# Turning attention output by crossbar DMA instead of TensorE in the later units of a fused sparse-attention and gated-FFN kernel

## The chip, the cores and the metric

The kernel runs on one core of one Trainium2 chip. The metric is the device time of one execution in microseconds (us), the median of several. A program on one core has no other core to wait for, so everything that sets the time is in one trace. The trace counts from the first to the last instruction and is about 2 us shorter than the device time: the profiled execution took 268.72 us and its span is 266.7 us.

Names used below: PE is TensorE's matmul side and PEld its weight load, DVE is VectorE, ACT is ScalarE, POOL is GpSimd, SP is SyncE. POOL issues software DMAs (q0), SP issues hardware DMAs (q1), crossbar transposes among them.

## The reference

Two layers, one after the other. The attention has 4 batches, 8 heads, 768 tokens and head size 64. Each query sees its neighbours within 16 positions, and 24 blocks of 32 tokens in a summarised form (keys by maximum, values by mean):

```python
k_sum = k.reshape(B, H, nb, block, D).max(axis=3)       # block = 32, nb = 24
v_sum = v.reshape(B, H, nb, block, D).mean(axis=3)
scores_l = scale * q @ k^T, only where |i - j| < 16
scores_s = scale * q @ k_sum^T + log(block)
a = softmax(concat(scores_l, scores_s));  x = a @ concat(v, v_sum)
```

The output x, as 3072 tokens by 512 features, goes through a gated feed-forward layer with a residual gate:

```python
g = x @ w_gate; val = x @ w_val                          # 512 -> 1536
ffn_out = (gelu(g) * val) @ w_out                        # 1536 -> 512
out = x + sigmoid(x @ w_res) * ffn_out
```

## The kernel before

The work is cut into 8 **units** of 384 tokens (half a batch each, numbered 0 to 7). Heads go in 4 **pairs** of 128 features. In the loop over `u`, the gated layer of unit `u` runs on TensorE with the attention of unit `n = u + 1` woven in, so that TensorE always has matmuls to do. `st` is the state of unit `u`, `nst` that of unit `n`.

Two things have to be turned (transposed) on the way. First, k and q of a batch come in as rows of tokens and are needed with features on the partitions. Second, the normalised attention output `xn` (tokens on partitions) has to become `xT` (features on partitions), since the gated layer contracts over features. TensorE can turn a 128x128 tile into PSUM, from where ACT copies it; SP can issue a crossbar DMA that turns from SBUF to SBUF.

```python
def load_rows(b):                       # rows of k, q (and v) of batch b, cast to bf16, one DMA per head
    for sb, src, name in ((k_sb, k, ..), (q_sb, q, ..), (v_sb, v, ..))[0:2 if b == 1 else 3]:
        ...
        for h in range(H) if b > 1 else (4, 5, 6, 7, 0, 1, 2, 3):
            nc.gpsimd.dma_start(out=sb[b][:, h // 2, :, ...], in_=src[b, h].rearrange("(c p) d -> p c d", c=NC))

def load_batch(b):                      # rows, then the values (vext) in 7 DMAs
    load_rows(b)
    for c in range(NC + 1): load_values(b, c)

def k_step(b, hp, pool, tag):           # turn a pair of k on TensorE: 6 transposes, ACT copy into kW, then
    tp = turn_pair(k_sb[b], hp, pool, tag)
    nc.scalar.copy(kw[:, :, OWN:OWN + QT]..., tp...)
    k_rest(kw)                          # five DVE operations: block maxima and the neighbours' columns
def q_step(...):                        # the same for q: 6 transposes and an ACT copy

def turn_batch(b, p0, p1):              # the same by crossbar DMA: two DMAs for k and one for q of a pair
    for hp in range(p0, p1):
        for e in range(2):
            nc.sync.dma_start_transpose(out=kt[:, :, e, OWN:OWN + QT], in_=k_sb[b][64 * e:64 * e + 64, hp]...)
        nc.sync.dma_start_transpose(out=qT[b % 2][hp]..., in_=q_sb[b][:, hp]...)
def turn_values(b): ...                 # 4 crossbar DMAs, v_sb -> vT, read by block_sums (a DVE reduction, vsT)

def xt_step(u, ko, st, pool, tag, copy):   # a pair of xn: 3 TensorE transposes and an ACT copy
    for sub in range(NSUB):
        nc.tensor.transpose(xp[:, sub * 128:(sub + 1) * 128], st["xn"][:, sub, ko * 128:(ko + 1) * 128], ident[:])
    copy(st["xT"][:, ko, :], xp[:])

def fo_step(st, gvT, fo):               # g and vv: 4 matmuls of 128x384 each (ko 0..3), then gelu (ACT), product (DVE)
def end_step(u, st, sub, c0=0, c1=DM):  # two DVE operations, then the store
    ...
    nc.sync.dma_start(out=out[row:row + 128, c0:c1], in_=o[:, 0:c1 - c0])
```

`ps_mm`, the pool of PSUM banks for g, vv, r and f, has 4 buffers. The loop, with cuts:

```python
for u in range(NU):
    if u == 1: turn_batch(1, 2, NP)                        # k, q of pairs 2 and 3 of batch 1 by crossbar DMA
    for fo in range(FO):                                   # 12 steps
        ... fo_step(st, gvT, fo); values_step(u, fo)       # block_sums, v_spread, vsum_bc at certain steps
        if u == 0 and fo == 4: ...; load_batch(1)
        if u == 2 and fo == 8: gate(gvT[0:1, fo, 0:1]); load_rows(3)     # gate: a POOL copy that waits for gvT
        if half == 0 and 1 < nb < B and fo == 0: vT[nb] = turn_values(nb); turn_batch(nb, 0, NP - 1)
        if half == 1 and 1 < nb < B and fo == 0: turn_batch(nb, NP - 1, NP)
        if half == 1 and 1 < nb < B and 1 < fo < 2 + NP: k_rest(kW[nb % 2][fo - 2])
        if u == 1 and fo == 6: gate(gvT[0:1, fo, 0:1]); load_batch(2)
        if u == 1 and fo in (0, 1, 4, 5): k_step of pairs 0, 1 (fo 0, 1); q_step of pairs 0, 1 (fo 4, 5)
        if u == 1 and fo >= FO - 2: k_rest(kW[1][fo - FO + NP])          # pairs 2, 3
    ...                                                    # u == 0 and u == 7 have their own endings
    s_step(n, 0, nst); s_step(n, 1, nst, ...)              # scores and exp
    res_step(st, 0); ffn_step(st, gvT, 0, 0, FO); res_step(st, 1)
    av_step(n, 0, nst, *AO); av_step(n, 1, nst, *TT)       # weighted values and normalisation: writes xn
    s_step(n, 2, nst); s_step(n, 3, nst, ..., masked=False)
    end_step(u, st, 0); mask_part(3, nst)
    ffn_step(st, gvT, 1, 0, 6);  xt_step(n, 0, ...);  ffn_step(st, gvT, 1, 6, FO);  xt_step(n, 1, ...)
    res_step(st, 2); av_step(n, 2, nst, *AO); av_step(n, 3, nst, *TT); end_step(u, st, 1)
    ffn_step(st, gvT, 2, 0, 7);  xt_step(n, 2, ...);  ffn_step(st, gvT, 2, 7, 10);  xt_step(n, 3, ...)
    ffn_step(st, gvT, 2, 10, FO); end_step(u, st, 2)
```

Of the kernel before, what the change touches and what calls it, by code (L numbers as in the profile page):

```python
# [8 lines left out]
F32 = mybir.dt.float32  # L9
BF16 = mybir.dt.bfloat16  # L10
# [5 lines left out]
def kernel(  # L16
# [86 lines left out]
    with tc.manual_schedule():  # L103
# [61 lines left out]
        def gate(t):  # L165
            nc.gpsimd.tensor_copy(tick[:], t)

        def load_rows(b):
            for sb, src, name in ((k_sb, k, "k_sb"), (q_sb, q, "q_sb"), (v_sb, v, "v_sb"))[0:2 if b == 1 else 3]:
                sb[b] = (qk1 if sb is v_sb else qk).tile([128, NP, NC, 2 * D], BF16, tag=name, name=name)  # L170
                for h in range(H) if b > 1 else (4, 5, 6, 7, 0, 1, 2, 3):
                    nc.gpsimd.dma_start(out=sb[b][:, h // 2, :, h % 2 * D:h % 2 * D + D],  # L172
                                        in_=src[b, h].rearrange("(c p) d -> p c d", c=NC))

# [158 lines left out]
        def av_norm(hp, st):  # L333
            ao = st["ao", hp]
            rz = work.tile([128, NSUB, 2, 1], F32, tag="rz", name="rz")
            nc.vector.reciprocal(rz[:], ao[:, :, :, D:D + 1])  # L336
            xn = st["xn"].rearrange("p s (h d) -> p s h d", d=D)[:, :, 2 * hp:2 * hp + 2, :]
            nc.vector.tensor_mul(xn, ao[:, :, :, 0:D], rz.to_broadcast([128, NSUB, 2, D]))  # L338

        def av_step(u, hp, st, pool=ps_o, tag="ao"):  # L340
# [3 lines left out]
        def xt_step(u, ko, st, pool, tag, copy=nc.vector.tensor_copy):  # L344
            xp = pool.tile([128, TU], BF16, tag=tag, name="xp")
            for sub in range(NSUB):
                nc.tensor.transpose(xp[:, sub * 128:(sub + 1) * 128],  # L347
                                    st["xn"][:, sub, ko * 128:(ko + 1) * 128], ident[:])
            copy(st["xT"][:, ko, :], xp[:])  # L349

        def new_unit():
            return {"xn": upool.tile([128, NSUB, DM], BF16, tag="xn", name="xn"),
                    "xT": upool.tile([128, KO, TU], BF16, tag="xT", name="xT")}

        def half_fo(st, w, fo, lo, hi, acc=None):
# [8 lines left out]
        def fo_end(gvT, fo, g, vv):  # L364
            ge = work.tile([128, TU], F32, tag="ge", name="ge")
            nc.scalar.activation(ge[:], g[:, 0:TU], AF.Gelu)  # L366
            nc.vector.tensor_mul(gvT[:, fo, :], ge[:], vv[:, 0:TU])  # L367
# [29 lines left out]
        def end_step(u, st, sub, c0=0, c1=DM):  # L397
            f, th = st["f", sub], st["th", sub][:, c0:c1]
            nc.vector.scalar_tensor_tensor(th, th, 1.0, f[:, 0:c1 - c0], ALU.add, ALU.mult)  # L399
            o = work.tile([128, DM], F32, tag="o", name="o")  # L400
            nc.vector.scalar_tensor_tensor(o[:, 0:c1 - c0], th, 0.5, st["xn"][:, sub, c0:c1], ALU.mult, ALU.add)  # L401
            row = u * TU + sub * 128
            nc.sync.dma_start(out=out[row:row + 128, c0:c1], in_=o[:, 0:c1 - c0])

        def keep_warm(n, wp=None):
            if wp is None:
# [79 lines left out]
        for u in range(NU):  # L486
            b, half = u // 2, u % 2
            nb = b + 1
            n = u + 1
            if u == 1:  # L490
                turn_batch(1, 2, NP)
            if u == 3:
                for c in range(NC + 1):
                    load_values(3, c)
            gvT = upool.tile([128, FO, TU], BF16, tag="gvT", name="gvT")
            for fo in range(FO):
                if u == 0 and fo < 2:
                    for w, _, acc in firsts[2 * fo:2 * fo + 2]:
                        half_fo(st, w, fo, KO - 1, KO, acc)
                    fo_end(gvT, fo, firsts[2 * fo][2], firsts[2 * fo + 1][2])  # L500
                else:
                    fo_step(st, gvT, fo)
                values_step(u, fo)
                if u == 0 and fo == 4:
                    nc.vector.memset(vsT[:], 0.0)
                    vext_consts(1)
                    kw_consts(1)
                    load_batch(1)
                if u == 2 and fo == 8:
                    gate(gvT[0:1, fo, 0:1])  # L510
                    load_rows(3)
                if half == 0 and 1 < nb < B and fo == 0:
                    vT[nb] = turn_values(nb)
                    turn_batch(nb, 0, NP - 1)
                if half == 1 and 1 < nb < B and fo == 0:
                    turn_batch(nb, NP - 1, NP)
                if half == 1 and 1 < nb < B and 1 < fo < 2 + NP:
                    k_rest(kW[nb % 2][fo - 2])
                if u == 1 and fo == 6:
                    gate(gvT[0:1, fo, 0:1])  # L520
                    load_batch(2)
                if u == 1 and fo in (0, 1, 4, 5):
                    home = TT if fo % 2 else AO
                    if fo < 4:
                        k_step(nb, fo, *home)
                    else:
                        q_step(q_sb[nb], nb, 0, S, fo - 4, *home)
                if u == 1 and fo >= FO - 2:
                    k_rest(kW[1][fo - FO + NP])
                if u == 0 and fo >= FO - 2:  # L530
                    for hp in range(2 * (fo - FO + 2), 2 * (fo - FO + 2) + 2):
                        q_step(qb, 0, TU, S, hp, *(TT if hp % 2 else AO))
            nst = new_unit() if n < NU else None
            if u == 0:
                s_step(n, 0, nst)
                s_step(n, 1, nst, two=(AO, TT))
                r = [res_part(st, sub) for sub in range(NSUB)]
                tanh_part(st, 0, r[0])
                tanh_part(st, 1, r[1])
# [12 lines left out]
                ffn_step(st, gvT, 1, 4, 8)  # L552
                ffn_step(st, gvT, 2, 0, 4)
                xt_step(n, 2, nst, *AO, nc.scalar.copy)
                xt_step(n, 3, nst, *TT, nc.scalar.copy)
                ffn_step(st, gvT, 2, 4, 8)
                for sub in range(NSUB):
                    ffn_step(st, gvT, sub, 8, FO)
                    end_step(u, st, sub)
                st = nst  # L560
                continue
            if nst is None:
                for sub in range(NSUB - 1):
                    res_step(st, sub)
                    ffn_step(st, gvT, sub, 0, FO)
                    end_step(u, st, sub)
                res_step(st, NSUB - 1)
                for c0, c1 in ((0, 256), (256, 384), (384, DM)):
                    ffn_step(st, gvT, NSUB - 1, 0, FO, c0, c1)
                    end_step(u, st, NSUB - 1, c0, c1)  # L570
                continue
            s_step(n, 0, nst)
            s_step(n, 1, nst, two=(AO, TT))
            res_step(st, 0)
            ffn_step(st, gvT, 0, 0, FO)
            res_step(st, 1)
            av_step(n, 0, nst, *AO)
            av_step(n, 1, nst, *TT)
            s_step(n, 2, nst)
            s_step(n, 3, nst, two=(MM, MM), masked=False)  # L580
            end_step(u, st, 0)
            mask_part(3, nst)
            ffn_step(st, gvT, 1, 0, 6)
            xt_step(n, 0, nst, *AO, nc.scalar.copy)
            ffn_step(st, gvT, 1, 6, FO)
            xt_step(n, 1, nst, *TT, nc.scalar.copy)
            res_step(st, 2)
            av_step(n, 2, nst, *AO)
            av_step(n, 3, nst, *TT)
            end_step(u, st, 1)  # L590
            ffn_step(st, gvT, 2, 0, 7)
            xt_step(n, 2, nst, *AO, nc.scalar.copy)
            ffn_step(st, gvT, 2, 7, 10)
            xt_step(n, 3, nst, *TT, nc.scalar.copy)
            ffn_step(st, gvT, 2, 10, FO)
            end_step(u, st, 2)
            st = nst
# [30 lines left out]
```

The softmax here doesn't subtract the row's maximum and nothing guards it: scores larger than these inputs give would overflow.

## Time and profile before

| What | Value |
|---|---|
| time, median of 3 runs (lowest to highest) | 268.97 us (268.72 to 269.71) |
| span of the profiled execution | 266.7 us |
| ACT busy | 136.2 us, 51% |
| POOL busy (mostly issuing DMAs, none after about 133 us) | 93.6 us, 35% |
| DMA queue of POOL (loads, cast to bf16) | 86,032 packets, 16.26 MB |
| DMA queue of SP (crossbar transposes and stores) | 26,464 packets, 11.80 MB |
| TensorE transposes of xn (`xp`, line 347) | 96 |
| crossbar transposes: kW, qT, vT | 20, 10, 8 |

How to read it: matmuls are pipelined, so the duration of one matmul in the profile (326 ns for 128x384) is longer than its share of a dense stream. What a matmul costs in the stream is the distance between starts. An engine that is not the bottleneck may idle for nothing; what counts is a gap on TensorE, and what ended it. The unit of the loop is the natural stage: it begins with the first g product of a unit.

### The profile page before, as it was taken

The page shows a single profiled execution, that of the slowest core. Times are in us where ns is not written, and L with a number is a line of the kernel's source. Part 1 is how long each engine was busy: PE and PEld are TensorE (multiplying, and loading weights), DVE is VectorE, ACT ScalarE, POOL GpSimd, SP SyncE. Part 2 cuts the span into 40 slices and gives each one's busy share as a digit, 9 for nine tenths or more (in the row PEclk, how much of TensorE's full clock was granted, in tenths as well). Part 3 has the DMA queues.
Part 4 walks back from the last instruction along what each step waited for, and adds up shares of the span by engine and source line. Part 5 has one row for each costly group of instructions (what it writes and reads, how often), then busy time and mean ns, then how long its engine had stood idle before and what let it go on. Part 6 is the DMA issues. An engine that isn't in the chain of part 4 may idle for free.

```text
span 266.7 us, 5803 instructions
## 1 busy us (share of the span) xinstructions
PE 253.3 (95%) x2275; PEld 142.9 (54%) x2300; DVE 174.4 (65%) x414; ACT 136.2 (51%) x236; POOL 93.6 (35%) x125
## 2 busy tenths in 40 slices
PE   8799999999999987999799999999999999999995
PEld 2546555566545544556455565556645565556544
DVE  3744853495597858877846789677837863664424
ACT  2756349645365534645265535745365536663310
POOL 7975542990999803999600000000000000000000
PEclk9999999999999999999999999999999999999999
DMA  5999999999999999999990275315001200020012
GB/s 84 170 169 196 197 206 186 136 176 141 165 129 146 177 141 140 129 181 198 155 72 7 106 141 98 68 42 138 0 4 39 81 0 2 0 90 32 0 42 79
DMA packets 112523, 28.43 MB, mean 107 GB/s; under 512 B 98672, under 2 KB 109552, under 8 KB 112496
## 3 DMA queue, kind: packets, MB, share of 16 engines
q0 software_dynamic: 86032, 16.26, 81.5%
q1 hardware_dynamic: 26464, 11.80, 21.4%
q8 instruction: 18, 0.29, 0.5%
q14 instruction: 9, 0.07, 0.1%
HBM read 32.51 MB, written 6.29 MB: 145 GB/s over the span
## 4 chain that ended last, share of the span: by engine, by line
PE 79%; DMA 9%; DVE 7%; issue 3%; ACT 1%; POOL 1%; DVEq 0%; POOLq 0%
PE f L394 22%; PE vv L360 19%; PE g L360 18%; PE r L378 7%; PE ao L328 3%; DMA vT<-v_sb 3%; DMA qa<-in_q_dram 3%; DMA kW<-k_sb 3%; PE s L296 3%; DVE gvT L367 2%; PE xp L347 2%; PE vs L254 1%; PE wp L409 1%; DVE vext L274 1%; DVE vsT L239 1%
## 5 line engine op out<-in xcount | busy, mean ns | idle before, releaser
L366 ACT ACTIVATE ge<-g 128x384 f32<-128x384 f32 x95 | 46.7, 491 | 66.4 <-PE g L360 37.1
L360 PE MATMUL vv<-xT,w_val 128*128 128x384 bf16 x380 | 77.8, 326 | 2.6 <-DVE gvT L367 2.6
L360 PE MATMUL g<-xT,w_gate 128*128 128x384 bf16 x380 | 77.8, 326 | 1.5 <-DVE gvT L367 1.5
L367 DVE TENSOR_TENSOR gvT<-ge,vv 128x384 bf16<-128x384 f32 x95 | 51.8, 550 | 31.7 <-PE vv L360 28.3
L394 PE MATMUL f<-w_out,gvT 128*128 128x512 bf16 (+2 forms) x298 | 68.6, 362 | 0.7
L360 PEld LDWEIGHTS <-w_val 128*128 128x128 bf16 x384 | 37.5, 98 | 28.7 <-issue 4.2
L360 PEld LDWEIGHTS <-w_gate 128*128 128x128 bf16 x384 | 37.0, 98 | 26.7 <-issue 2.2
L394 PEld LDWEIGHTS <-gvT 128*128 128x128 bf16 x312 | 27.6, 98 | 25.6
L349 ACT COPY xT<-xp 128x384 bf16<-128x384 bf16 x32 | 15.1, 481 | 22.6 <-PE xp L347 22.6
L378 PE MATMUL r<-w_res,xT 128*128 128x512 bf16 x88 | 23.6, 380 | 0.6 <-issue 0.3
L399 DVE SCALAR_TENSOR_TENSOR th<-th,f 128x512 f32<-128x512 f32 (+2 forms) x26 | 16.7, 641 | 11.4 <-PE f L394 8.5
L99 POOL DMA_DIRECT2D vext<-in_v_dram x28 | 23.3, 870 | 2.1 <-PE g L360 1.7
L172 POOL DMA_DIRECT2D k_sb<-in_k_dram x24 | 20.0, 850 | 10.2 <-DMA w_out<-in_moe_w_out_dram 5.2
L384 ACT ACTIVATE th<-r 128x512 f32<-128x512 f32 x24 | 14.2, 602 | 17.9 <-PE r L378 17.9
L313 DVE TENSOR_TENSOR P<-P,maskt 128x768 bf16<-128x768 bf16 x28 | 15.4, 555 | 10.0 <-ACT P L305 7.7
L172 POOL DMA_DIRECT2D q_sb<-in_q_dram x24 | 20.0, 856 | 0.4 <-DMA k_sb<-in_k_dram 0.2
L338 DVE TENSOR_TENSOR xn<-ao,rz 128x384 bf16<-128x384 f32 x32 | 17.8, 557 | 1.1
L305 ACT ACTIVATE P<-s,bias_t 128x768 bf16<-128x768 f32 x18 | 16.2, 903 | 3.8 <-PE s L296 3.7
L401 DVE SCALAR_TENSOR_TENSOR o<-th,xn 128x512 f32<-128x512 f32 (+2 forms) x26 | 16.9, 650 | 0.9
L336 DVE RECIPROCAL rz<-ao 128x6 f32<-128x6 f32 x32 | 6.1, 190 | 15.7 <-PE ao L328 15.7
L302 ACT ACTIVATE P<-s,bias_t 128x384 bf16<-128x384 f32 x28 | 14.6, 578 | 0.0
L172 POOL DMA_DIRECT2D v_sb<-in_v_dram x16 | 13.2, 869 | 0.2 <-issue 0.2
(82 smaller groups left out, 212.5 us busy)
## 6 DMA issues: line engine op xcount, KB each, us to landing
out_dram<-o SPq DMA_DIRECT2D x23, 256.0 KB, 2.1
vext<-in_v_dram POOLq DMA_DIRECT2D x20, 128.0 KB, 7.8
k_sb<-in_k_dram POOLq DMA_DIRECT2D x24, 96.0 KB, 6.1
q_sb<-in_q_dram POOLq DMA_DIRECT2D x24, 96.0 KB, 4.3
w_gate<-in_moe_w_gate_dram POOLq DMA_DIRECT2D x6, 256.0 KB, 8.9
w_val<-in_moe_w_val_dram POOLq DMA_DIRECT2D x6, 256.0 KB, 9.1
w_out<-in_moe_w_out_dram POOLq DMA_DIRECT2D x3, 512.0 KB, 14.1
v_sb<-in_v_dram POOLq DMA_DIRECT2D x16, 96.0 KB, 6.3
```

The lines of the kernel that those rows point to most:

```text
L99: nc.gpsimd.dma_start(out=dst, in_=v[b, :, lo:hi, :].rearrange("h p d -> p h d"))
L172: nc.gpsimd.dma_start(out=sb[b][:, h // 2, :, h % 2 * D:h % 2 * D + D], in_=src[b, h].rearrange("(c p) d -> p c d", c=NC))
L305: nc.scalar.activation(P.rearrange("p a t q -> p a (t q)"), s[:, :, 0:TU], AF.Exp, scale=scale, bias=bias_t[:])
L313: nc.vector.tensor_mul(Pf, Pf, maskt.unsqueeze(1).to_broadcast([128, 2 * HT, QT]))
L338: nc.vector.tensor_mul(xn, ao[:, :, :, 0:D], rz.to_broadcast([128, NSUB, 2, D]))
L360: nc.tensor.matmul(acc[:, 0:TU], w[:, ko, fs], st["xT"][:, ko, :], start=(ko == 0), stop=(ko == KO - 1))
L366: nc.scalar.activation(ge[:], g[:, 0:TU], AF.Gelu)
L367: nc.vector.tensor_mul(gvT[:, fo, :], ge[:], vv[:, 0:TU])
L378: nc.tensor.matmul(r[:], st["xT"][:, ko, ss], w_res[:, ko, :], start=(ko == 0), stop=(ko == KO - 1))
L394: nc.tensor.matmul(st["f", sub][:, 0:c1 - c0], gvT[:, fo, ss], w_out[:, fo, c0:c1], start=(fo == 0), stop=(fo == FO - 1))
L399: nc.vector.scalar_tensor_tensor(th, th, 1.0, f[:, 0:c1 - c0], ALU.add, ALU.mult)
L401: nc.vector.scalar_tensor_tensor(o[:, 0:c1 - c0], th, 0.5, st["xn"][:, sub, c0:c1], ALU.mult, ALU.add)
```

## The change

For units 4 to 7 the first three pairs of the attention output are turned by crossbar DMA instead of TensorE and ACT. That DMA takes time to land, so the first three products of these units contract pairs 0, 1 and 3 first and pair 2 last; pair 3 stays on TensorE. `xn` is laid out by pairs so that the source of a transpose is contiguous. So that SP's in-order queue doesn't hold the transposes behind stores, the stores of units 3 to 6 go by POOL's software queue. In return the crossbar no longer turns k and q of pairs 2 and 3 of batch 1: TensorE turns all four pairs of them in unit 1, the heads are loaded in plain order, and the load of batch 2 is issued at the start of unit 1 with no gate.

```diff
-                for h in range(H) if b > 1 else (4, 5, 6, 7, 0, 1, 2, 3):
+                for h in range(H):
...
+        def xt_dma(ko, st):
+            nc.sync.dma_start_transpose(out=st["xT"][:, ko, :].rearrange("d (s m) -> d s m", s=NSUB),
+                                        in_=st["xn"][:, ko].rearrange("p s d -> p (s d)"))
...
-            return {"xn": upool.tile([128, NSUB, DM], BF16, tag="xn", name="xn"),
+            return {"xn": upool.tile([128, KO, NSUB, 128], BF16, tag="xn", name="xn"),
...
-            nc.sync.dma_start(out=out[row:row + 128, c0:c1], in_=o[:, 0:c1 - c0])
+            (nc.gpsimd if 2 < u < NU - 1 else nc.sync).dma_start(out=out[row:row + 128, c0:c1], in_=o[:, 0:c1 - c0])
...
             if u == 1:
-                turn_batch(1, 2, NP)
+                load_batch(2)
...
+            if u > 3:
+                firsts = [(w, fo, ps_mm.tile([128, 512], F32, tag="mm", name="gv"))
+                          for w, fo in ((w_gate, 0), (w_val, 0), (w_gate, 1))]
+                for kos in ((0, 1, 3), (2,)):
+                    for w, fo, acc in firsts:
+                        for ko in kos:
+                            nc.tensor.matmul(acc[:, 0:TU], w[:, ko, ...], st["xT"][:, ko, :],
+                                             start=(ko == 0), stop=(ko == 2), skip_group_check=True)
...
-                if u == 1 and fo == 6:
-                    gate(gvT[0:1, fo, 0:1])
-                    load_batch(2)
-                if u == 1 and fo in (0, 1, 4, 5):
+                if u == 1 and fo < 8:
                     home = TT if fo % 2 else AO
-                    (k_step of pairs 0, 1 at fo 0, 1; q_step of pairs 0, 1 at fo 4, 5)
-                if u == 1 and fo >= FO - 2:
-                    k_rest(kW[1][fo - FO + NP])
+                    (k_step of pairs 0 to 3 at fo 0 to 3; q_step of pairs 0 to 3 at fo 4 to 7)
...
+            if u < 3:  (the ending as before)
+            else:
+                xt_dma(0, nst)
+                xt_dma(1, nst)
+                mask_part(3, nst)
+                end_step(u, st, 0)
+                ffn_step(st, gvT, 1, 0, FO)
+                av_step(n, 2, nst, *AO)
+                xt_dma(2, nst)
+                av_step(n, 3, nst, *TT)
+                res_step(st, 2)
+                end_step(u, st, 1)
+                ffn_step(st, gvT, 2, 0, 10)
             xt_step(n, 3, nst, *TT, nc.scalar.copy)
             ffn_step(st, gvT, 2, 10, FO)
             end_step(u, st, 2)
```

The lines in brackets stand for code that is cut.

More of the change, by code (lines that the diff above doesn't have):

```diff
@@ L336, in av_norm @@
             nc.vector.reciprocal(rz[:], ao[:, :, :, D:D + 1])
-            xn = st["xn"].rearrange("p s (h d) -> p s h d", d=D)[:, :, 2 * hp:2 * hp + 2, :]
+            xn = st["xn"][:, hp].rearrange("p s (h d) -> p s h d", d=D)
             nc.vector.tensor_mul(xn, ao[:, :, :, 0:D], rz.to_broadcast([128, NSUB, 2, D]))
@@ L347, in xt_step @@
                 nc.tensor.transpose(xp[:, sub * 128:(sub + 1) * 128],
-                                    st["xn"][:, sub, ko * 128:(ko + 1) * 128], ident[:])
+                                    st["xn"][:, ko, sub, :], ident[:])
             copy(st["xT"][:, ko, :], xp[:])
+        def xt_dma(ko, st):
+            nc.sync.dma_start_transpose(out=st["xT"][:, ko, :].rearrange("d (s m) -> d s m", s=NSUB),
+                                        in_=st["xn"][:, ko].rearrange("p s d -> p (s d)"))
         def new_unit():
-            return {"xn": upool.tile([128, NSUB, DM], BF16, tag="xn", name="xn"),
+            return {"xn": upool.tile([128, KO, NSUB, 128], BF16, tag="xn", name="xn"),
                     "xT": upool.tile([128, KO, TU], BF16, tag="xT", name="xT")}
@@ L400, in end_step @@
             o = work.tile([128, DM], F32, tag="o", name="o")
-            nc.vector.scalar_tensor_tensor(o[:, 0:c1 - c0], th, 0.5, st["xn"][:, sub, c0:c1], ALU.mult, ALU.add)
+            nc.vector.scalar_tensor_tensor(o[:, 0:c1 - c0].rearrange("p (k d) -> p k d", d=128),
+                                           th.rearrange("p (k d) -> p k d", d=128), 0.5,
+                                           st["xn"][:, c0 // 128:c1 // 128, sub, :], ALU.mult, ALU.add)
             row = u * TU + sub * 128
-            nc.sync.dma_start(out=out[row:row + 128, c0:c1], in_=o[:, 0:c1 - c0])
+            (nc.gpsimd if 2 < u < NU - 1 else nc.sync).dma_start(out=out[row:row + 128, c0:c1], in_=o[:, 0:c1 - c0])
         def keep_warm(n, wp=None):
@@ L495 @@
             gvT = upool.tile([128, FO, TU], BF16, tag="gvT", name="gvT")
+            if u > 3:
[4 more added lines that the diff above has]
+                        for ko in kos:
+                            nc.tensor.matmul(acc[:, 0:TU], w[:, ko, fo * 128:(fo + 1) * 128], st["xT"][:, ko, :],
+                                             start=(ko == 0), stop=(ko == 2), skip_group_check=True)
             for fo in range(FO):
@@ L500 @@
                     fo_end(gvT, fo, firsts[2 * fo][2], firsts[2 * fo + 1][2])
+                elif u > 3 and fo == 0:
+                    fo_end(gvT, fo, firsts[0][2], firsts[1][2])
+                elif u > 3 and fo == 1:
+                    fo_end(gvT, fo, firsts[2][2], half_fo(st, w_val, fo, 0, KO))
                 else:
@@ L518 @@
                     k_rest(kW[nb % 2][fo - 2])
-                if u == 1 and fo == 6:
-                    gate(gvT[0:1, fo, 0:1])
-                    load_batch(2)
-                if u == 1 and fo in (0, 1, 4, 5):
+                if u == 1 and fo < 8:
                     home = TT if fo % 2 else AO
-                    if fo < 4:
-                        k_step(nb, fo, *home)
-                    else:
-                        q_step(q_sb[nb], nb, 0, S, fo - 4, *home)
-                if u == 1 and fo >= FO - 2:
-                    k_rest(kW[1][fo - FO + NP])
+                    hp, kq = fo % NP, fo // NP
+                    if kq:
+                        q_step(q_sb[nb], nb, 0, S, hp, *home)
+                    else:
+                        k_step(nb, hp, *home)
                 if u == 0 and fo >= FO - 2:
@@ L580 @@
             s_step(n, 3, nst, two=(MM, MM), masked=False)
[L581 to L593, printed above, removed]
+            if u < 3:
+                end_step(u, st, 0)
+                mask_part(3, nst)
+                ffn_step(st, gvT, 1, 0, 6)
+                xt_step(n, 0, nst, *AO, nc.scalar.copy)
+                ffn_step(st, gvT, 1, 6, FO)
+                xt_step(n, 1, nst, *TT, nc.scalar.copy)
+                res_step(st, 2)
+                av_step(n, 2, nst, *AO)
+                av_step(n, 3, nst, *TT)
+                end_step(u, st, 1)
+                ffn_step(st, gvT, 2, 0, 7)
+                xt_step(n, 2, nst, *AO, nc.scalar.copy)
+                ffn_step(st, gvT, 2, 7, 10)
+            else:
+                xt_dma(0, nst)
+                xt_dma(1, nst)
+                mask_part(3, nst)
+                end_step(u, st, 0)
+                ffn_step(st, gvT, 1, 0, FO)
+                av_step(n, 2, nst, *AO)
+                xt_dma(2, nst)
+                av_step(n, 3, nst, *TT)
+                res_step(st, 2)
+                end_step(u, st, 1)
+                ffn_step(st, gvT, 2, 0, 10)
             xt_step(n, 3, nst, *TT, nc.scalar.copy)
```

## The prediction

> **What bounds the kernel now.** I read first the busy shares and the chain of the page, to find the engine that sets the end:
>
> ```profile
> PE 253.3 (95%) x2275; PEld 142.9 (54%) x2300; DVE 174.4 (65%) x414; ACT 136.2 (51%) x236; POOL 93.6 (35%) x125
> ...
> PE 79%; DMA 9%; DVE 7%; issue 3%; ACT 1%; POOL 1%; DVEq 0%; POOLq 0%
> ```
>
> TensorE is busy 95% of the span and 79% of the chain. So there are two ways to gain: fewer instructions on TensorE, or shorter gaps on it, which are 266.7 - 253.3 = 13.4 us in all. The view by windows, cut at the first g product of each unit, shows where the gaps lie (columns: window, its length, busy time of PE, PEld, DVE, ACT, POOL with their counts, then clock, DMA share, GB/s):
>
> ```profile
> 54.80:87.34 32.54, 32.05 (x281) 18.25 (x283) 24.58 (x58) 17.49 (x31) 25.92 (x33) 1.00 1.92 152
> 87.34:119.62 32.28, 29.54 (x255) 16.36 (x257) 25.03 (x46) 16.24 (x29) 19.87 (x25) 1.00 1.81 153
> 119.62:150.24 30.62, 28.92 (x250) 16.23 (x252) 20.42 (x50) 15.64 (x28) 10.80 (x14) 1.00 1.38 105
> 150.24:179.50 29.26, 29.00 (x254) 16.39 (x256) 23.74 (x46) 16.19 (x29) 0.00 (x0) 1.00 0.46 96
> 179.50:208.41 28.91, 28.75 (x250) 16.25 (x252) 19.78 (x50) 15.68 (x28) 0.00 (x0) 1.00 0.16 42
> 208.41:237.28 28.87, 28.71 (x250) 16.25 (x252) 17.89 (x36) 15.64 (x28) 0.00 (x0) 1.00 0.07 28
> ```
>
> These are units 1 to 6. Units 5 and 6 are dense: 0.16 us of gap each. Unit 2 has 32.28 - 29.54 = 2.74 us of gap and unit 3 has 1.70 us. Unit 1 is long because it has more matmuls, and has 0.49 us of gap. Then I asked DVE's waits what made the gaps:
>
> ```profile
> DVE vsT L239 <- DMA vT<-v_sb: 3.4, 2, 2.2
> DVE km L206 <- DMA kW<-k_sb: 1.2, 1, 1.2
> ```
>
> In unit 2, DVE waits for the crossbar transpose of v before the block sums. The products gvT stand behind these in DVE's queue, and TensorE waits for their PSUM banks. In unit 3 the same comes of the last pair of k. In both cases the transposes were slow because POOL's loads were in flight. The first vT, issued at 89.6 us, landed after 8.5 us; in unit 4, with no loads, the same transposes landed in 2.8 us.
>
> **What the Trainium skill says.** "VectorE: DVE Perf Modes", section "The three transpose paths", gives 390 ns for a 128x128 transpose on TensorE and 1309 ns on the crossbar. Here a lone TensorE transpose shows 219 ns, and three of them between matmuls cost 0.17 us, that is 57 ns each in the stream. For the crossbar this trace shows 1.2 us of issue and 2.8 us to landing for six tiles at once. "DMA: Bandwidth & Descriptors", section "Issuing engines are not separate DMA queues", says DMAs of all issuers run on the same 16 engines and interleave; the 8.5 us against 2.8 us agrees. "SBUF — State Buffer", section "Who interferes with whom", says a DVE copy in a two-port mode and GpSimd block each other. The same column copy (L210) took 0.48 us while POOL was issuing at 58.57 us, and 0.20 us at 60.47 us after POOL had stopped. That agrees, though it is no proof of the cause.
>
> **Part 1: k and q of pairs 2 and 3 on TensorE, unit 1.** Four more turns of 6 transposes are 24 x 57 ns = **+1.37 us** on TensorE. ACT gets four more copies of 0.80 us; with one gelu of 0.49 us a step that is 1.3 us, under the 1.64 us that TensorE then needs for a step (8 x 163 ns + 6 x 57 ns). DVE is nearer the limit. Its five operations for a pair of k now come in four consecutive steps, and this is how the first two went:
>
> ```profile
> 57.25 0.55 DVE L367 TENSOR_TENSOR gvT<-ge,vv 128x384 bf16<-128x384 f32 x1
> 57.72 0.35 DVE L206 TENSOR_TENSOR km<-kW 128x384 bf16<-128x384 bf16 x1
> 58.10 0.55 DVE L208 TENSOR_REDUCE ks<-km 128x24 bf16<-128x384 bf16 x1
> 58.57 0.48 DVE L210 COPY kW<-kW 128x176 bf16<-128x176 bf16 x1
> 58.69 0.41 DVE L211 COPY kW<-kW 128x176 bf16<-128x176 bf16 x1
> 59.02 0.21 DVE L212 COPY kW<-ks 128x288 bf16<-128x288 bf16 x1
> 59.16 0.54 DVE L367 TENSOR_TENSOR gvT<-ge,vv 128x384 bf16<-128x384 f32 x1
> ```
>
> From one gvT to the next is 1.91 us, so DVE loses 0.27 us a step, 1.1 us over four. The four PSUM banks let vv of step fo + 2 run once gvT of step fo is done. By these starts vv of step 4 begins at about 62.0 us and needs gvT 2 at 61.5; vv of step 6 begins at 65.3 us and needs gvT 4 at 65.3. So TensorE is touched only at the end: +0.3 us. The two pairs' operations that stood at steps 10 and 11 are gone from there, which may give back up to 0.3 us (one wait of TensorE for a masked P, 0.2 us). Unit 1: **+1.4 us**.
>
> **Part 2: the earlier load of batch 2.** Before, POOL idled from 59.56 us (end of the values of batch 1) to the gate at 66.12 us. Without the gate the 31 loads start 6.6 us earlier, and issue back to back at 0.83 us each, if their completions allow it. Before, the last values were issued at 90.8 to 92.3 us, across the start of vT's transposes. In the changed kernel they go out by about 85.7 us. Unit 2 starts at about 88.8 us, and the transposes of v come 2.2 us later, behind the last store. They then find few loads in flight and should land in 3 to 5 us, before the block sums of step 5 at about 98 us. The gap of unit 2 should shrink to what unit 4, the same code with no loads, shows: 0.26 us. **-2.5 us** in the gap; with fewer slowed DVE copies I take -2.6 us.
>
> **Part 3: unit 3.** The load of batch 3 is gated on step 8 of unit 2 in both kernels. It takes some 28 us of issue, and the last pair of k is turned 2 us into unit 3, some 20 us after the gate: still among the loads. I keep 1.4 of the 1.7 us gap: **-0.3 us**.
>
> **Part 4: xT by crossbar, endings of units 3 to 6.** Each loses 9 transposes: 9 x 57 ns = 0.51 us, four times: **-2.05 us**. The question is whether pair 2 lands in time. In the ending of unit 5, moved to the new order, TensorE does 12 f matmuls from 201.08 us (216 ns each), then the values of pair 2 by 203.95. DVE does the mask of pair 3 (to 203.4), the two operations of the end (0.69 us each, to 204.8), the reciprocal and xn, done by 205.6. Six tiles land in 2.8 us; three tiles, an estimate from that, in about 2.5: 208.2 us. The new first products start at 207.8 us; 9 matmuls x 163 ns later, at 209.26, pair 2 is needed. Slack is 1 us. Pair 3 is tighter: its ACT copy ends about 208.05 us and its first matmul is due at 208.13. I add +0.3 us over all four units for these. Stores by POOL (0.33 us of issue on SP before, 2.0 us to landing) may overlap the transpose; they are 256 KB in 2 KB rows, so I expect tenths of a microsecond, inside the slack.
>
> **The sum:** +1.4 - 2.6 - 0.3 - 2.05 + 0.3 = -3.25 us, so 268.97 - 3.25 = **265.7 us**, 1.2% faster.
>
> **Rivals.**
> First, **the earlier load only moves the queue**. The page shows DMA engines at 9 tenths through units 0 to 2. If they are truly full, loads land no earlier, vT waits as before, and part 2 gives nothing: about 268.3 us. For it: the digit. Against it: POOL issued loads from 66 us on with no wait, and q's landed in 3.3 to 3.9 us there, so the engines kept up; and six crossbar transposes leave unit 1.
> Second, **pair 2 lands late**. If a transpose beside a store takes 5 us, TensorE waits some 1.5 us in each of four units: +6 us, 271.7 us. For it: loads stretched transposes to 7 and 8 us. Against it: those were long trains of packets under 512 bytes, and one store is 2 us of large ones.
> Third, **DVE becomes the bound of unit 1**. If POOL's issuing slows each pair's operations to 2.4 us a step, DVE loses 3 us over four steps and TensorE waits some 2 us: 267.5 us.
> Fourth, **unit 3's gap vanishes too**, if loads of batch 3 get ahead: 264.3 us.
>
> **Range and chances.** The savings on TensorE (2.05 us) and the cost (1.37 us) are counted instructions and nearly sure; unit 2's gap is the largest uncertain term (0 to -2.7 us), then lateness of pair 2 (0 to +6, most likely under 0.5), unit 1 (0 to +2) and unit 3 (0 to -1.7). Together 263.7 to 268.3 us, 8 times in 10. Over 2% faster means under 263.6 us: all terms good at once. Over 2% slower, over 274.3 us, would need the second rival at its worst.
>
> **What would show it.** Right: unit 1 some 33.9 us long; unit 2 about 29.6 us with DVE no longer waiting for vT; units 5 and 6 about 28.4 us, with no wait of TensorE for xT at the first products; unit 3 still waiting for kW. Wrong: a wait "gv from DMA xT" in units 4 to 7; gvT late in steps 3 to 6 of unit 1; vT still landing in over 6 us in unit 2; or unit 4 slowed, where SP issues 13 other transposes.

## The result, and the profile after

The changed kernel takes 264.75 us (264.24 to 265.45) against 269.33 us for the kernel before, timed beside it. The ratio is 0.9834, 95% interval 0.9802 to 0.9866: 1.7% faster. The span went from 266.7 to 262.5 us.

The busy shares and the chain of waits of the changed kernel, from its page:

```profile
PE 251.4 (96%) x2263; PEld 142.0 (54%) x2288; DVE 174.8 (67%) x414; ACT 133.2 (51%) x228; POOL 100.1 (38%) x136
...
PE 86%; DMA 6%; POOL 3%; issue 1%; DVE 1%; ACT 1%; POOLq 0%; DVEq 0%
```

TensorE is busy 1.9 us less, and its share of the chain rose from 79 to 86%, DVE's fell from 7 to 1%. So 4.2 - 1.9 = 2.3 us, more than half of what the span gained, are waits that went. TensorE's waits for the product gvT, behind which a PSUM bank comes free, fell from 4.1 to 1.2 us (two lines of before, one of after; us in total, times, longest):

```profile
PE vv L360 <- DVE gvT L367: 2.6, 4, 1.1
PE g L360 <- DVE gvT L367: 1.5, 1, 1.5
PE g L364 <- DVE gvT L371: 1.2, 1, 1.2
```

The windows, cut at the first product of units 1 to 6 (window, its length, busy time of PE, PEld, DVE, ACT, POOL, then clock, DMA share, GB/s), say where:

```profile
54.82:88.10 33.28, 33.12 (x305) 19.50 (x307) 25.25 (x58) 20.30 (x35) 30.15 (x37) 1.00 1.83 142
88.10:117.40 29.30, 29.04 (x254) 16.39 (x256) 24.92 (x46) 16.25 (x29) 15.76 (x20) 1.00 1.61 154
117.40:147.12 29.72, 28.37 (x242) 15.75 (x244) 20.18 (x50) 14.31 (x25) 10.88 (x15) 1.00 1.77 112
147.12:175.91 28.79, 28.53 (x245) 15.88 (x247) 23.75 (x46) 14.79 (x26) 1.63 (x4) 1.00 0.61 107
175.91:204.30 28.39, 28.23 (x242) 15.76 (x244) 19.74 (x50) 14.22 (x25) 1.65 (x4) 1.00 0.21 54
204.30:232.70 28.40, 28.24 (x242) 15.74 (x244) 17.91 (x36) 14.19 (x25) 1.62 (x4) 1.00 0.12 39
```

| Unit | before, us | after, us | difference | predicted |
|---|---|---|---|---|
| 1 | 32.54 | 33.28 | +0.74 | +1.4 |
| 2 | 32.28 | 29.30 | -2.98 | -2.6 |
| 3 | 30.62 | 29.72 | -0.90 | -0.3 (gap) - 0.51 (transposes) |
| 4 | 29.26 | 28.79 | -0.47 | -0.51 |
| 5 | 28.91 | 28.39 | -0.52 | -0.51 |
| 6 | 28.87 | 28.40 | -0.47 | -0.51 |

What stands before unit 1 is the same (54.80 and 54.82 us). The last unit is 0.38 us longer, all of it after TensorE's last matmul; more on that below. The sum is -4.2 us, the difference of the spans.

In the view of DVE's waits, the line of `vsT` that waited for vT is gone. The one of `km` stays:

```profile
DVE km L206 <- DMA kW<-k_sb: 1.1, 1, 1.1
```

### The profile page after: what moved, and what is told of

It is laid out like the page before. It is cut to its first block, busy times and chain, and to the rows that moved or that the text cites. A ratio compares the mean times of both kernels' runs of the same rounds, so it can differ in the third digit from the quotient of the medians.

```text
span 262.5 us, 5776 instructions
## 1 busy us (share of the span) xinstructions
PE 251.4 (96%) x2263; PEld 142.0 (54%) x2288; DVE 174.8 (67%) x414; ACT 133.2 (51%) x228; POOL 100.1 (38%) x136
## 4 chain that ended last, share of the span: by engine, by line
PE 86%; DMA 6%; POOL 3%; issue 1%; DVE 1%; ACT 1%; POOLq 0%; DVEq 0%
PE f L398 23%; PE vv L364 21%; PE g L364 20%; PE r L382 8%; PE ao L328 4%; PE gv L508 3%; DMA vext<-in_v_dram 3%; DMA kW<-k_sb 3%; PE s L296 2%; POOL vext L99 2%; PE xp L347 1%; PE tp L185 1%; PE vs L254 1%; PE gv L364 1%; POOL k L90 1%
## 5 line engine op out<-in xcount | busy, mean ns | idle before, releaser
L364 PE MATMUL vv<-xT,w_val 128*128 128x384 bf16 x364 | 74.5, 326 | 0.0
L370 ACT ACTIVATE ge<-g 128x384 f32<-128x384 f32 x87 | 42.8, 492 | 59.5 <-PE g L364 33.9
L364 PE MATMUL g<-xT,w_gate 128*128 128x384 bf16 x348 | 71.3, 326 | 1.2 <-DVE gvT L371 1.2
L371 DVE TENSOR_TENSOR gvT<-ge,vv 128x384 bf16<-128x384 f32 x91 | 49.6, 551 | 27.9 <-PE vv L364 26.3
L398 PE MATMUL f<-w_out,gvT 128*128 128x512 bf16 (+2 forms) x298 | 66.6, 362 | 0.7
L364 PEld LDWEIGHTS <-w_val 128*128 128x128 bf16 x368 | 36.0, 98 | 24.5 <-issue 0.9
L364 PEld LDWEIGHTS <-w_gate 128*128 128x128 bf16 x352 | 33.8, 98 | 23.3 <-issue 1.8
L409 POOL DMA_DIRECT2D out_dram<-o x12 | 6.6, 546 | 98.8 <-DVE rz L336 83.9
L398 PEld LDWEIGHTS <-gvT 128*128 128x128 bf16 x312 | 28.3, 98 | 28.2
L349 ACT COPY xT<-xp 128x384 bf16<-128x384 bf16 x20 | 9.3, 482 | 17.5 <-PE xp L347 17.5
```

The costliest lines, as they stand in the source:

```text
L364: nc.tensor.matmul(acc[:, 0:TU], w[:, ko, fs], st["xT"][:, ko, :], start=(ko == 0), stop=(ko == KO - 1))
L398: nc.tensor.matmul(st["f", sub][:, 0:c1 - c0], gvT[:, fo, ss], w_out[:, fo, c0:c1], start=(fo == 0), stop=(fo == FO - 1))
```

## The experiments

Lengths of units are compared where the clock of the window is 1.00. In some profiles TensorE ran at a lower clock for a few microseconds, in the first 20 us or after a gap; the last section says what the traces show of this.

### Was it the earlier load of batch 2? The gate put back

```diff
-            if u == 1:
-                load_batch(2)
...
+                if u == 1 and fo == 6:
+                    gate(gvT[0:1, fo, 0:1])
+                    load_batch(2)
```

> The changed kernel with the load of batch 2 put back behind its gate at step 6 of unit 1; everything else stays. Theory A (the load that starts 7 us earlier closed the gap of unit 2): the transposes of v meet the loads again and land in 6 to 9 us, unit 2 grows from 29.3 to about 31.8 us, the time from 264.8 to about 267.3 us. Rival B (the six crossbar transposes that left unit 1 freed the DMA engines, and the gate did not matter): unit 2 stays under 30 us and the time at about 265 us.

Measured: 268.63 us, 0.9971 of the kernel before (0.9947 to 0.9995). Its second unit, in the view by windows, and DVE's wait:

```profile
89.18:121.53 32.35, 29.54 (x254) 16.37 (x256) 25.52 (x46) 16.21 (x29) 20.28 (x26) 1.00 1.74 155
```

```profile
DVE vsT L239 <- DMA vT<-v_sb: 2.9, 1, 2.9
```

The gap is back (2.81 us), and so is the wait for vT, whose transposes landed after 5.8 to 9.3 us instead of 2.8 to 5.0. The unit is as long as before the change, although the six crossbar transposes of unit 1 were gone here. Rival B falls: without the earlier load the gap stays. The time is 1.3 us above theory A's number. This profile is 1.1 us longer before unit 1, at a lower clock, but the 14 runs at a clock of 0.999 or more have a median of 268.4 us too, so the clock does not explain it; what does stays open.

### Is the earlier load enough? It alone, on the kernel before

```diff
             if u == 1:
                 turn_batch(1, 2, NP)
+                load_batch(2)
...
-                if u == 1 and fo == 6:
-                    gate(gvT[0:1, fo, 0:1])
-                    load_batch(2)
```

> The kernel before with one edit: the load of batch 2 at the start of unit 1, ungated; k and q of pairs 2 and 3 stay on the crossbar and xT stays on TensorE. Theory A (the earlier load closes the gap of unit 2): unit 2 falls from 32.3 to about 29.7 us, unit 1 stays at 32.3 to 32.8 us, time about 266.5 us. Rival B (fewer crossbar transposes in unit 1 did it): unit 2 stays at about 32 us and the time near 269 us; the crossbar transposes of unit 1 might also land too late for the scores, which would lengthen unit 1.

> The kernel before with the early ungated load of batch 2 alone, once more, since the clock of TensorE was lowered to 0.95 in units 2 and 3 of its first profile. If the six crossbar transposes of unit 1 slow the loads enough that these end 4 us into unit 2 (as in the first profile), the gap of unit 2 is again 2 to 3 us and the time 268 to 269 us. If the loads end by the start of unit 2, the gap is under 0.6 us and the time about 266.5 us.

Measured: 267.73 us, ratio 0.9947 (0.9926 to 0.9969), and the second time 267.55 us, 0.9941 (0.9916 to 0.9965). In the first profile the values went out only at 91.24 us, 4.1 us into unit 2; DVE waited 3.7 us for vT, and TensorE 2.56 us for gvT, after which its clock was lower for some 4 us. Where the load came out so late, it gained nothing. The second profile has the full clock; its unit 2 and the wait:

```profile
87.18:117.76 30.58, 29.67 (x258) 16.36 (x256) 24.56 (x46) 16.23 (x29) 18.06 (x24) 1.00 1.66 154
```

```profile
DVE vsT L239 <- DMA vT<-v_sb: 1.7, 1, 1.7
```

There the load alone shortens unit 2 by 1.7 us of the 3.0. Neither number of the second expectation is right: the gap is 0.91 us, between the under 0.6 and the 2 to 3 that it named. The medians put the gain in time at 1.3 and 1.5 us (269.0 and 269.09 us for the kernel before). POOL's timeline shows why. In the profile of the changed kernel its values go out like this (start, length, engine, line, count):

```profile
68.73 6.58 POOL L172 DMA_DIRECT2D q_sb<-in_q_dram  x8
75.22 6.86 POOL L172 DMA_DIRECT2D v_sb<-in_v_dram  x8
82.02 5.79 POOL L99 DMA_DIRECT2D vext<-in_v_dram  x7
```

With the early load but the crossbar transposes of k and q still in unit 1 (second profile), q's loads wait for older loads to complete, and the last values go out later:

```profile
75.22 0.82 POOL L172 DMA_DIRECT2D q_sb<-in_q_dram  x1 [0.62 <-DMA k_sb<-in_k_dram]
76.24 1.64 POOL L172 DMA_DIRECT2D q_sb<-in_q_dram  x2 [0.20 <-issue]
77.86 3.31 POOL L172 DMA_DIRECT2D v_sb<-in_v_dram  x4
81.40 3.28 POOL L172 DMA_DIRECT2D v_sb<-in_v_dram  x4 [0.23 <-DMA q_sb<-in_q_dram]
84.65 5.77 POOL L99 DMA_DIRECT2D vext<-in_v_dram  x7
```

There they are out at 90.42 us, here at 87.81. The bracket on a line names what POOL waited for.

### Both at once: k and q of pairs 2 and 3 back on the crossbar

```diff
             if u == 1:
+                turn_batch(1, 2, NP)
                 load_batch(2)
...
-                if u == 1 and fo < 8:
+                if u == 1 and fo in (0, 1, 4, 5):
...
+                if u == 1 and fo >= FO - 2:
+                    k_rest(kW[1][fo - FO + NP])
```

> The changed kernel with k and q of pairs 2 and 3 of batch 1 back on the crossbar (heads 4 to 7 loaded first, block maxima at steps 10 and 11), the early ungated load kept. If the two parts are independent: unit 1 falls from 33.3 to about 32.4 us and unit 2 stays at 29.3, time about 264.0 us, a version faster than both. Rival (the crossbar transposes of unit 1 and the early load share the DMA engines and hinder each other): unit 2's gap comes back in part or the scores of unit 2 wait at the end of unit 1, time 265 to 266.5 us.

Measured: 266.85 us, ratio 0.9883 (0.981 to 0.9956). Unit 1 falls to 32.55 us, 0.73 less than in the changed kernel, as expected. But unit 2 is 29.84 us with a gap of 0.55, DVE waits 1.0 us for vT, and unit 3 is 30.26 us with DVE waiting 2.0 us for kW. What unit 1 gives, units 2 and 3 take back: 0.54 + 0.54 us. Unit 1 also starts 1.3 us later in this profile, at a lower clock before it. That is not why the median is 2.1 us over the changed kernel's: the two runs with the clock at 0.999 are the longest of the four (267.14 and 268.25 us), and with four runs this stays open. The parts are not independent, and this version isn't shown to be better.

Six profiles stand in one order, by how long after the start of unit 2 POOL was done with issuing the values:

| Kernel | values issued by, against the start of unit 2 | length of unit 2, us |
|---|---|---|
| before | 92.26 - 87.34 = +4.9 us | 32.28 |
| gate put back | 94.01 - 89.18 = +4.8 us | 32.35 |
| earlier load alone, first profile | 91.24 - 87.10 = +4.1 us | 33.71, about 1.7 of it matmuls at half speed after the gap |
| earlier load alone, second profile | 90.42 - 87.18 = +3.2 us | 30.58 |
| k and q back on the crossbar | 90.82 - 88.64 = +2.2 us | 29.84 |
| changed | 87.81 - 88.10 = -0.3 us | 29.30 |

The transposes of v, issued some 2.2 us into the unit, come late as far as the loads of the values overlap them. The three profiles with the earlier load and the crossbar transposes run the same program up to there, save for the layout of xn, so their spread is one of executions: the removed gate takes 0.8 to 2.7 us off that overlap. With the six crossbar transposes out of unit 1 besides, the spread is gone: in the seven other profiles that have both edits and the same ending of unit 2, the values are out 0.4 to 1.6 us before unit 2 and it takes 29.29 to 29.30 us. Against the second profile of the load alone, the loads end 2.6 us earlier in the changed kernel, and the unit starts 0.9 us later, most of it TensorE's added work. That added work is what pays for the rest of the gain.

### xT on TensorE again

```diff
-            if u < 3:
+            if u < NU:
                 end_step(u, st, 0)
```

with the plain order of the first products and all stores on SP.

> The changed kernel with x of all pairs turned on TensorE again in the endings of units 3 to 6, the plain order of the first products, and all stores on SP; the early load and TensorE's k and q of unit 1 stay. Theory C (the gain of these units is the 9 transposes of 57 ns that TensorE no longer does): units 3 to 6 longer by 0.5 us each, time about 266.8 us. Rival D (something else helped there, as the ACT copies that went or the stores that moved): the units change by clearly less or more than 0.5 us each. If the last unit, 29.80 us long in the changed kernel against 29.42 before, goes back to 29.4, the POOL stores made its tail longer.

Measured: 266.26 us, ratio 0.9858 (0.9779 to 0.9937). Units 4 to 6 of this kernel:

```profile
147.13:176.43 29.30, 29.04 (x255) 16.38 (x256) 23.76 (x46) 16.24 (x29) 0.00 (x0) 1.00 0.48 96
176.43:205.30 28.87, 28.71 (x251) 16.25 (x253) 19.79 (x50) 15.65 (x28) 0.00 (x0) 1.00 0.16 42
205.30:234.17 28.87, 28.71 (x251) 16.25 (x253) 17.90 (x36) 15.64 (x28) 0.00 (x0) 1.00 0.08 28
```

They are 0.51, 0.48 and 0.47 us longer than in the changed kernel, which is 9 transposes of 57 ns. TensorE's busy time differs by as much (0.51, 0.48, 0.47 us) and its gaps by nothing, so the ACT copies and the stores, which this run undoes as well, have no part in it. In unit 3 the difference is 0.25 us, because the gap there differs too; that is one reason why the time is under the 266.8 us expected. Theory C holds for units 4 to 6. The last unit is 29.83 us with all stores on SP, so POOL's stores are not what makes its tail longer. Over all profiles the last unit takes 29.35 to 29.83 us, and no run separated a cause.

### The stores back on SP

```diff
-            (nc.gpsimd if 2 < u < NU - 1 else nc.sync).dma_start(out=out[...], in_=o[...])
+            nc.sync.dma_start(out=out[...], in_=o[...])
```

> The changed kernel with the stores of units 3 to 6 back on SP's queue; the transposes of xn stay there too. The change moved the stores so that SP, which issues in order, would not hold a transpose behind a store. Theory E (the order in the program already keeps the transposes ahead: the first store is ready about 0.8 us before xn of pair 2, and a store takes 0.33 us of SP): no wait appears, units 3 to 6 stay within 0.1 us, time within 0.5 us of the changed kernel. Rival F (the stores hold the transposes): a wait of TensorE for xT of pair 2 at the first products of units 4 to 7, 0.5 to 1.5 us each, time up to 4 us more.

Measured: 264.02 us, ratio 0.983 (0.9794 to 0.9866), the same as the changed kernel's. SP's timeline at the end of unit 5 shows the order that the program gives:

```profile
200.73 0.33 SPq L409 DMA_DIRECT2D out_dram<-o  x1
201.43 1.18 SPq L352 DMA_TRANSPOSE xT<-xn  x1
```

The first store is issued 0.7 us before the third transpose, which waits for xn, not for the store. Units 4 and 5 are 28.79 and 28.37 us. Unit 6 is 28.53, 0.13 more than in the changed kernel: the first matmul of pair 2 starts 0.2 us after its turn there. With the stores on POOL the same unit varies from 28.40 to 28.82 us, so this is no cost of SP. Moving the stores to POOL brought nothing.

### The plain order of the first products

The edit takes out the block `if u > 3: firsts = ...` and its two branches at steps 0 and 1.

> The changed kernel with the plain order of the first products (pairs 0, 1, 2, 3, one product after the other) in units 4 to 7. In the trace of the changed kernel the last of the three transposes of a unit is issued 2.4 us before its first product and lands 2.3 us after issue when no store is in flight, up to 4.1 us beside one. Theory G (the reordering is needed): TensorE waits 0.3 to 1.5 us for xT of pair 2 at the first g of units 4 to 7, time 1 to 4 us more. Rival H (it lands in time anyway): units within 0.1 us of the changed kernel.

Measured: 266.30 us, ratio 0.9906 (0.9876 to 0.9935). TensorE's timeline at the start of unit 6:

```profile
204.88 0.49 PE L364 MATMUL g<-xT,w_gate 128*128 128x384 bf16 x2
206.56 0.48 PE L364 MATMUL g<-xT,w_gate 128*128 128x384 bf16 x2 [1.20 <-DMA xT<-xn]
```

After pairs 0 and 1 it waits 1.20 us for pair 2. In unit 4 it waits 0.35 us, in units 5 and 7 not at all. Both theories were too simple: the order is needed in some units. The third transpose was issued at 202.5 us and took 4.1 us to land. In the changed kernel it took 3.9 us at this place (issued at 201.9 us), and by the starts in the windows above pair 2 was due there 9 x 163 ns after 204.3 us, at 205.8. The reordering is worth just what that landing needs.

### The same for unit 3, among loads

```diff
-            if u < 3:
+            if u < 2:
...
-            if u > 3:
+            if u > 2:
```

> The changed kernel with xT of pairs 0 to 2 by crossbar one unit more, for unit 3 as well (the ending of unit 2), where the loads of batch 3 are in flight. If loads stretch these transposes as they stretched those of k and v (7 to 9 us to landing instead of 2.4), TensorE waits 2 to 5 us at the first products of unit 3 and the time is 266.5 to 269.5 us: then the change stops at unit 4 because of the loads. If the transposes land in under 4 us in spite of the loads, the time falls by another 0.5 us to about 264.2 us.

Measured: 267.47 us, ratio 0.9934 (0.9912 to 0.9957). The three transposes landed after 6.5 to 7.7 us, and TensorE's waits show

```profile
PE gv L508 <- DMA xT<-xn: 3.5, 2, 2.3
```

both at the start of unit 3. Unit 2 is 0.44 us shorter (28.86), unit 3 is 34.02 us, part of that at a lower clock after these gaps. This is the prediction's second rival one unit earlier, with loads in the place of the store: beside loads the crossbar is late, which is a reason for the change to stop at unit 4.

### The last pair of batch 2 turned one unit earlier

```diff
-                    turn_batch(nb, 0, NP - 1)
+                    turn_batch(nb, 0, NP if nb == 2 else NP - 1)
-                if half == 1 and 1 < nb < B and fo == 0:
+                if half == 1 and 2 < nb < B and fo == 0:
                     turn_batch(nb, NP - 1, NP)
```

> The changed kernel with the last pair of k and q of batch 2 turned by the crossbar in unit 2, behind the other three, instead of at the start of unit 3. The gap of unit 3 (1.35 us in the changed kernel) is a wait of DVE for that transpose among the loads of batch 3. Theory I (the transpose starts too late): issued near 109 us it lands by about 117 us, before its block maxima at about 126 us; the wait goes, unit 3 falls from 29.7 to about 28.6 us, time about 263.7 us. Rival J (more transposes in unit 2 delay the loads of batch 3 or hold the stores behind them): unit 2 or unit 3 grows by as much, time 264.5 to 266 us.

Measured: 263.81 us, ratio 0.9832 (0.9785 to 0.9879). Unit 3 of this kernel:

```profile
117.17:145.54 28.37, 28.21 (x242) 15.75 (x244) 19.85 (x50) 14.32 (x25) 10.65 (x15) 1.00 1.51 115
```

1.35 us less than in the changed kernel, the whole gap; unit 2 is unchanged at 29.30 us. The transposes still took 6.7 us to land among the loads, but 10 us ahead of their use. Theory I holds for the unit. Unit 6, which the edit doesn't touch, is 0.42 us longer (28.82 us): pair 2 landed after 4.3 us there, and its first matmul, due 9 x 163 ns after 202.70 us, at 204.17, starts at 204.62 (`PE gv L508 <- DMA xT<-xn: 0.3, 1, 0.3`). By time the gain isn't clear of the spread in this run.

### Together, and against the changed kernel on one chip

> The changed kernel with both edits that helped or cost nothing: the last pair of k and q of batch 2 turned in unit 2, and all stores on SP. Additive theory: unit 3 at 28.4 us as with the first edit alone, units 4 to 6 at 28.8, 28.4, 28.4 us, about 1.3 us (0.5%) under the changed kernel run beside it. Rival: the pair turned earlier and the stores on one queue hinder each other, no more than 0.5 us under it.

> As the one before it, and the first store of each ending is issued after the transpose of pair 2 instead of before it. The transpose of pair 2 landed after 2.3 us with no store in flight and after up to 4.3 us beside one. If the store in flight is what stretches it: its landing is 2.3 to 2.8 us in all four units, no wait of TensorE at the first products, time equal to or up to 0.3 us under the one before it. If something else stretches it (loads, the other transposes): landings of 3 to 4 us stay.

> The changed kernel itself, on the same chip as the two versions above, for a comparison on one chip: about 1.7% under the kernel before, the two versions above about 0.5% under this one.

The first is the pair turned in unit 2 and all stores on SP. The second also issues the first store of an ending after the transpose of pair 2. The third is the changed kernel.

| Kernel | us, median (lowest to highest) | ratio to before (95%) | unit 3, us |
|---|---|---|---|
| pair 3 in unit 2, stores on SP | 263.15 (262.67 to 263.35) | 0.9782 (0.9751 to 0.9813) | 28.66 |
| and the store after the transpose | 263.29 (262.52 to 264.28) | 0.9791 (0.9760 to 0.9822) | 28.97 |
| changed kernel | 264.77 (263.88 to 266.08) | 0.9849 (0.9815 to 0.9883) | 29.08 |

The first is 263.15 / 264.77 = 0.994 of the changed kernel, and no run of it was as long as the shortest of the changed kernel. It is the best version found. DVE's wait for kW is gone in both, yet unit 3 is not at the 28.37 us of the edit alone: in the second, TensorE still waits 0.43 us for gvT, where DVE's small copies into kW (L211, L212) took 0.57 and 0.53 us instead of 0.20 while POOL was issuing. Part of the 0.6% can't be read from these single profiles, in which unit 3 of the changed kernel had a gap of 0.55 us instead of 1.35: how long that gap is differs from execution to execution.

What stretches the transpose of pair 2? The later store does not cure it: at the end of unit 5 its landing isn't recorded, but the first matmul of pair 2 starts 3.91 us after the issue (200.95 to 204.86 us), as it does after 3.92 us in the changed kernel. The traces point to something else. In ten profiles the endings of units 3 to 6 have 118 recorded landings of these transposes. In 76 of them no packet of the queue that the page calls q8, instruction, was in flight, and all took 2.28 to 2.44 us, 27 of these beside a store. All the longer landings, 2.65 to 4.30 us, had one of its 16 KB packets in flight, one of them (3.68 us) with no store. The DMA view of the changed kernel from 201.87 to 205.75 us, where pair 2 took 3.88 us, has it:

```profile
q8 instruction: 1, 0.02, 1.5%
```

No run moved this packet, so the tie is seen in every landing but not tested by an edit.

## Why the prediction was right or wrong

The prediction was 265.7 us, the time 264.75; 3.25 us were forecast and 4.2 came in the spans (4.6 in the medians). Its steps:

- **Part 1, unit 1, +1.4 forecast, +0.74 measured.** The transposes cost 4 x 0.33 = 1.3 us as counted. The term "+0.3 us" for DVE was wrong: no wait for gvT shows in unit 1, since gvT followed gvT after 1.6 to 2.1 us in the steps with the pairs' operations, close to the 1.91 taken, and the four banks bore it. And what left steps 10 and 11 gave more than the 0.2 us wait for a masked P: those values' matmuls also ran 0.28 us faster (0.85 before, 0.57 after), because the mask was ready. Some 0.6 us in all, of which part varies: with the early load alone, these operations still in place, one profile of unit 1 took 32.19 us and the other 32.53.
- **Part 2, -2.6 forecast, -2.98 measured.** The size was right, the reason half right. I put the gain down to the removed gate, and named the six crossbar transposes only as a point against the first rival. The runs show it needs both: with the transposes left in, the early load gave unit 2 nothing, 1.7 and 2.4 us in three profiles; the transposes' removal alone gave nothing. "Back to back at 0.83 us, by about 85.7 us" failed as well: POOL stood three times, 2.7 us in all, and the values were out at 87.8 us, 0.3 us before unit 2, the closest of eight profiles. That it sufficed was closer than I thought. A reading was wrong too: the loads of q before, taken as a sign that the engines kept up, landed in 3.3 to 5.1 us, not 3.3 to 3.9.
- **Part 3, -0.3 forecast.** After the 0.51 us of the transposes, unit 3 gained 0.39 us in this profile, and 1.03 us in the second profile of the changed kernel. The wait stayed, as said. The pair turned in unit 2 shows what most of it was: DVE's wait for kW.
- **Part 4, -0.51 a unit, -0.47 to -0.52 measured** in units 4 to 6, and confirmed by its undoing. The allowance of 0.3 us for lateness was not needed in this profile (under 0.1 us, in unit 6), but it was about right: in nine profiles with the reordered products pair 2 came 0 to 0.45 us late in unit 6, and once 0.1 us late in unit 4. "Slack is 1 us" was mis-sized in the landing: pair 2 was issued 3.9 us before its use, as counted (3.7), but took 3.2 to 4.3 us there and not the 2.5 estimated wherever a packet of q8 was in flight; most transposes took 2.3.
- **The last unit, +0.38 us,** stood in no part. Part 1 and part 2 came out 0.7 and 0.4 us better than forecast, so the sum is near for errors that this one offset in part.
- **The rivals.** "The earlier load only moves the queue" was true where the transposes of unit 1 stayed, in part. "Pair 2 lands late" is 2 to 3 us only beside loads; in the plain order it is 1.20 us in one unit, with the new order up to 0.45. The third, DVE as the bound of unit 1, did not come. The fourth, unit 3's gap vanishing, came in part in the second profile of the changed kernel: 0.55 us instead of 1.35.

## What to carry to other kernels

A transfer that is waited for late in a queue is late because of what is in flight when it starts, so ask when the foreign loads end, not when they begin; both an earlier issue and less traffic beside them count, and here neither alone was enough in every execution. A crossbar transpose off TensorE is worth what TensorE's transposes cost in a dense stream (57 ns here), provided that it starts some 4 us ahead even in a quiet place (landings there: 2.3 to 4.3 us). Among loads the landings took 5 to 10 us here, so start it 10 us ahead, as with the pair turned in unit 2.

## What the runs showed of the hardware that I had not expected

A crossbar transpose of three 128x128 tiles took SP as long to issue as one of six (1.2 us each), and landed in 2.3 against 2.8 us with no loads in flight. Between these two sizes its time is mostly fixed.

A gap on TensorE can cost more than itself. In the first profile of the earlier load alone, a wait of 2.01 us in unit 3 is followed by matmuls at half speed (start, length, count; a group of four in a dense stream takes 0.81 us):

```profile
134.68 0.81 PE L360 MATMUL g<-xT,w_gate 128*128 128x384 bf16 x4 [2.01 <-DVE gvT L367]
135.33 1.31 PE L360 MATMUL vv<-xT,w_val 128*128 128x384 bf16 x4
136.44 1.49 PE L360 MATMUL g<-xT,w_gate 128*128 128x384 bf16 x4
137.72 1.40 PE L360 MATMUL vv<-xT,w_val 128*128 128x384 bf16 x4
138.96 0.81 PE L360 MATMUL g<-xT,w_gate 128*128 128x384 bf16 x4
```

From 135.33 to 138.96 three groups take 3.63 us instead of 3 x 0.65 = 1.95, so this wait cost 1.7 us more. The same follows the waits of 2.56 us in unit 2 there and of 2.25 us among loads. But the length of the wait alone doesn't decide it. The second profile of the same kernel has a wait as long at the same place, and the matmuls go on at full speed:

```profile
131.65 0.81 PE L360 MATMUL g<-xT,w_gate 128*128 128x384 bf16 x4 [2.02 <-DVE gvT L367]
132.29 0.81 PE L360 MATMUL vv<-xT,w_val 128*128 128x384 bf16 x4
```

After 1.81 us (gate put back), after 1.54 us (unit 3 before) and after 1.20 us (plain order) nothing was lost either. What decides it, and over which stretch the idle time counts, was not measured.
